# Two blocks of a feed-forward stage cut into slices of 4, 10, 12 and 6 steps, with accumulating stores, and a fixed order for the first attention block

## The chip, the cores and the metric

The kernel runs on one core of a Trainium2 chip. Its time is the device time of one execution in microseconds (us). Five engines run side by side, each with its own queue of instructions: TensorE (PE in the profile, PEld for its weight loads), VectorE (DVE), ScalarE (ACT), GpSimd (POOL) and SyncE (SP), which only issues DMA transfers here. DMA transfers are also issued from ACT's queue.

## The reference

A banded attention feeds a first feed-forward stage (FFN 1), and that a second one (FFN 2). What matters of it:

```python
# attention: 4 batches, 8 heads, 576 positions, 64 wide; 2304 tokens in all
scores = scale * q @ k.T; masked to a window of 32 (heads 0-3)
                          or to every 4th of 128 (heads 4-7)
attn = softmax(scores); x = attn @ v            # x: 2304 x 512
# FFN 1, d_ff 2048
h = x @ w_in
g = where(h > 0, h, exp(min(h, 0)) - 1)
x = g @ w_out
# FFN 2, d_ff 1536
out = ((x @ w_a) * (x @ w_b)) @ w_out2
```

All inputs arrive as float32.

## The kernel before

**Blocks and steps.** The tokens are cut into six blocks of 384 (`TB`). A block's x has four tiles, one for each pair of heads (p = 0 to 3, called head 0 to 3 from here on), and each is kept as a high and a low part. FFN 1 runs in steps (block t, slice f of 128 of the 2048 hidden columns), 16 slices for each block, 96 steps in all; the list `STEPS1` gives their order. A step s has an input pass `h1_mm` (12 matmuls of 128x384 into one of two `ps_h` banks, line 603; three for each tile of x, as high and low parts are combined), then `el` and `g` (ACT: relu and exp, lines 624 and 625; DVE: line 630; ACT and POOL split it into parts, lines 614 and 615), and two steps later its output pass `y1_mm` (12 matmuls into four `ps_y` banks, line 649). When the run of steps of one block ends, `y1_out` copies the four banks out.

**The order of the blocks.** The list runs block 0 through slices 0 to 6 (`SPLIT` = 7), block 1 through all 16, block 0 through slices 7 to 15, then blocks 2 to 5 whole. Block 0's first part is stored to a buffer `yp` in DRAM; `y_part_load` brings it back later, DVE adds it to the second part, and SP stores the sum. So block 1's steps 7 to 13 use slices whose weights are already in place.

**Weights.** A chunk of weights (1i f: the slice's input weights, 1o f: its output weights, 512 KB each) is loaded by `w_load` into one of four `wraw` buffers and converted: on ACT two passes (lines 273, 278), on DVE clamp, join and sign (lines 283, 288, 291), on ACT the high part (line 299), on DVE the low part (line 318). Chunks up to slice 7 (1i up to 9) are converted at a fixed place, two in each step, behind that step's g (`at_step(st, "C", w_convert, ...)`). The others are broken into single operations (`chunk_ops`); a planner (`tick`, two in a step) lets them out by a budget of each engine's time (`ROOM1` up to step `C0`, then `ROOM`), and after them the preparation of FFN 2's weights, which go back to DRAM.

**Attention of blocks 0 and 1.** For each head: `early_scores` (one mask matmul, line 407, and small matmuls, line 421), `early_exp` (kind "V": DVE takes the maximum and subtracts, ACT does one exponential; kind "A": DVE takes the maximum, ACT does six small exponentials with sums), `early_norm` (sum and reciprocal on DVE, the product on POOL, line 462), `early_transpose` (three transposes, line 470, and a copy on ACT, line 473) and `early_values` (small matmuls, line 488, into two `ps_a` banks of two; ACT takes the high part, line 503, DVE the low part, line 504). Block 0's four heads come before step 0 in a loop, shifted against each other. Block 1's heads are laid by the list `B1` into steps 0 to 6, those of block 2 by `B2` from step 18 on.

**What sets the order.** The engines' queues are in order; the order in them is chosen when the program is built, from the order in which the code is written and from when operands are expected. `tc.issue_after(x)` puts an instruction behind x on the same engine's queue, without a wait between engines. PE runs 11 matmuls on zeros ahead of the first scores (`warm`); `keep_warm` puts more of them around block 0's last two heads.

## Time and profile before

| | us |
|---|---|
| median of 3 runs | 906.41 (906.32 to 907.79) |
| the profiled execution | 904.56 |
| its span, first to last instruction | 902.5 |
| PE busy | 883.1 (98%) |
| DVE busy | 650.7 (72%) |
| ACT busy | 504.6 (56%) |
| POOL busy | 270.5 (30%) |

A row of the profile's timeline gives the start, the duration, the engine, the line of the kernel, the operation with the tiles that it writes and reads, the shapes, and the number of instructions; in brackets stands how long the engine sat idle ahead of it and what ended that. The duration of a row of matmuls counts the tail of the last one, so rows that follow each other overlap a little. PEclk is TensorE's granted clock as a share of 2.4 GHz.

### The profile page before, as it was taken

The numbers are of one execution on the slowest core, as the hardware profiler recorded it, in microseconds if no ns is written. First come the engines' busy times: TensorE is split into PE (matmuls) and PEld (weight loads), VectorE is DVE, ScalarE is ACT, GpSimd is POOL, SyncE is SP. The second block draws the span as 40 slices with busy tenths as digits, with TensorE's granted clock in tenths as the row PEclk, the third lists the DMA queues.
The fourth block names the chain that finished last, engine by engine and source line by source line (L and its number), as shares of the span: only waits on it lengthen the run. The fifth ranks groups of instructions, "written<-read, shape, count | busy, mean of one in ns | idle before, by whom it ended". The sixth has DMA issues, their size and how long they took to land.

```text
span 902.5 us, 17842 instructions
## 1 busy us (share of the span) xinstructions
PE 883.1 (98%) x6648; PEld 850.5 (94%) x6648; DVE 650.7 (72%) x1126; ACT 504.6 (56%) x1235; POOL 270.5 (30%) x252
## 2 busy tenths in 40 slices
PE   8989998999999999999999999999999999999998
PEld 5778998899999999999989999999999999999998
DVE  5899988777777776777865466689756689656666
ACT  5898787777677777676656342325342225343231
POOL 1132332333333333332222122222522222522233
PEclk8999999999999999999999999999999999999999
DMA  9575453748646655537996687766787754687722
GB/s 352 186 260 198 142 161 121 261 160 271 203 163 221 213 186 208 187 130 249 345 326 213 219 298 259 250 221 202 239 324 251 245 199 164 229 297 245 245 71 70
DMA packets 76245, 198.18 MB, mean 220 GB/s; under 512 B 8320, under 2 KB 22656, under 8 KB 76160
## 3 DMA queue, kind: packets, MB, share of 16 engines
q1 hardware_dynamic: 64064, 178.05, 58.3%
q10 hardware_dynamic: 12096, 19.01, 5.8%
q8 instruction: 52, 0.85, 0.4%
q14 instruction: 33, 0.27, 0.1%
HBM read 153.51 MB, written 43.52 MB: 218 GB/s over the span
## 4 chain that ended last, share of the span: by engine, by line
PE 81%; DVE 7%; ACT 2%; DMA 1%; issue 1%; ACTq 0%; SPq 0%; DVEq 0%
PE ps_h L1051 28%; PE ps_y L649 18%; PE ps_h L603 17%; PE ps_o L1380 14%; PE ps_v L586 1%; PE ps_s L550 1%; PE ps_t L570 1%; PE ps_o L1240 1%; DVE wt L288 1%; DVE wt L291 1%; DVE wraw L994 1%; DMA w<-w2Q__2948 1%; DMA w<-w2P_b 1%; ACT el L625 0%; DMA w2P_a<-wraw 0%
## 5 line engine op out<-in xcount | busy, mean ns | idle before, releaser
L1051 PE MATMUL ps_h<-y,w 128*128 128x384 f32 x1512 | 291.4, 336 | 0.0
L1051 PEld LDWEIGHTS ps_h<-y,w 128*128 128x128 f32 x1512 | 256.2, 188 | 2.1 <-DVE el L1106 0.6
L603 PE MATMUL ps_h<-x,w 128*128 128x384 f32 x1152 | 223.9, 340 | 4.1 <-DVE el L630 3.0
L649 PE MATMUL ps_y<-g,w 128*128 128x384 f32 x1152 | 223.0, 339 | 1.9 <-DVE w L318 0.8
L603 PEld LDWEIGHTS ps_h<-x,w 128*128 128x128 f32 x1152 | 198.7, 188 | 9.1 <-DVE el L630 4.2
L615 POOL TENSOR_TENSOR g<-el,g 128x384 fp32r<-128x384 f32 x96 | 116.5, 1214 | 298.4 <-ACT g L614 242.9
L649 PEld LDWEIGHTS ps_y<-g,w 128*128 128x128 f32 x1152 | 199.5, 188 | 5.9 <-DVE w L318 1.4
L1380 PE MATMUL ps_o<-w,g 128*128 128x256 f32 x1071 | 152.8, 281 | 1.3 <-DVE g L1168 1.3
L1380 PEld LDWEIGHTS ps_o<-w,g 128*128 128x128 f32 x1071 | 146.6, 188 | 2.0 <-DVE g L1168 1.8
L630 DVE SCALAR_TENSOR_TENSOR el<-el,ps_h 128x384 f32<-128x384 f32 x96 | 53.0, 552 | 80.1 <-ACT el L625 80.1
L624 ACT ACTIVATE el<-ps_h 128x384 f32<-128x384 f32 x96 | 46.7, 487 | 53.2 <-PE ps_h L603 49.5
L1093 POOL TENSOR_TENSOR g<-el,g 128x384 fp32r<-128x384 f32 x34 | 38.8, 1141 | 123.2 <-ACT g L1092 106.5
L1403 DVE TENSOR_TENSOR acc<-acc,ps_o 128x512 f32<-128x512 f32 (+1 forms) x77 | 49.6, 644 | 34.3 <-PE ps_o L1380 34.0
L288 DVE SCALAR_TENSOR_TENSOR wt<-wt,wraw 128x512 uint32<-128x512 uint32 x68 | 60.1, 889 | 3.3 <-ACT wraw L278 1.2
L291 DVE SCALAR_TENSOR_TENSOR wt<-wraw,wt 128x512 uint32<-128x512 uint32 x68 | 61.2, 905 | 0.9
L614 ACT ACTIVATE g<-el 128x384 fp32r<-128x384 f32 x96 | 49.6, 516 | 15.2 <-DVE el L630 15.2
L625 ACT ACTIVATE el<-el 128x384 f32<-128x384 f32 x96 | 50.2, 524 | 1.9
L278 ACT ACTIVATE wraw<-wraw 128x512 uint32<-128x512 uint32 x68 | 45.4, 669 | 6.7 <-issue 2.0
L273 ACT ACTIVATE wt<-wraw 128x512 f32<-128x512 f32 x68 | 44.8, 661 | 4.2 <-DMA wraw<-in_w1i 3.1
L1102 ACT COPY el<-ps_h 128x384 f32<-128x384 f32 x36 | 17.3, 479 | 53.3 <-PE ps_h L1051 51.0
L1141 DVE TENSOR_TENSOR u<-ps_h,u 128x384 f32<-128x384 f32 x36 | 20.0, 557 | 35.2 <-PE ps_h L1051 35.1
L1122 ACT COPY u<-ps_h 128x384 f32<-128x384 f32 x36 | 17.3, 480 | 47.2 <-PE ps_h L1051 47.2
(116 smaller groups left out, 1036.1 us busy)
## 6 DMA issues: line engine op xcount, KB each, us to landing
w<-w2P_o SPq DMA_DIRECT2D x52, 512.0 KB, 5.3
w<-w2P_a SPq DMA_DIRECT2D x48, 512.0 KB, 4.3
w<-w2P_b SPq DMA_DIRECT2D x48, 512.0 KB, 4.4
wraw<-in_w1i SPq DMA_DIRECT2D x16, 512.0 KB, 5.1
wraw<-in_w1o SPq DMA_DIRECT2D x16, 512.0 KB, 4.0
wraw<-in_w2a SPq DMA_DIRECT2D x12, 512.0 KB, 3.7
wraw<-in_w2b SPq DMA_DIRECT2D x12, 512.0 KB, 3.9
wraw<-in_w2o SPq DMA_DIRECT2D x12, 512.0 KB, 3.7
```

The costliest lines, as they stand in the source:

```text
L288: V.scalar_tensor_tensor(t, t, 3, L, op0=ALU.logical_shift_left, op1=ALU.bitwise_or)
L291: V.scalar_tensor_tensor(t, H, 0x80000000, t, op0=ALU.bitwise_and, op1=ALU.bitwise_or)
L603: T.matmul(ps[:, :TB], w[:, wi, kc * 128 : (kc + 1) * 128], xs[kc][:, xi, :], start=(n == 0), stop=(n == 3 * KC - 1),)
L614: A.activation(g[:, 0, :], gf, AF.Copy)
L615: G.tensor_tensor(g[:, 1, :], gf, f32(g[:, 0, :]), op=ALU.subtract)
L624: A.activation(e, ps[:, :TB], AF.Relu, scale=-1.0)
L625: last_e[0] = A.activation(e, e, AF.Exp, scale=-1.0)
L630: last_g[0] = V.scalar_tensor_tensor(e, e, -1.0, h_ps.pop(s)[:, :TB], op0=ALU.add, op1=ALU.max)
L649: T.matmul(y_ps[t][c][:, :TB], w[:, wi, c * 128 : (c + 1) * 128], g[:, gi, :], start=(first and n == 0), stop=(last and n == 2),)
L1051: last_mm[0] = T.matmul(ps[:, :TB], w[:, wi, kc * 128 : (kc + 1) * 128], y2[S, yop][kc][:, xi, :], start=(start and n == 0), stop=(n == 5) ...
L1380: T.matmul(ps[:, 256 * n : 256 * n + 256], g[name][:, gi, i * 128 : (i + 1) * 128], w[:, wi, h, :], start=((first or not held) and n == m ...
L1403: V.tensor_tensor(a, a, ps[:, :n], op=ADD)
```

## The change

The order of FFN 1's first two blocks becomes block 0 slices 0 to 3, block 1 slices 0 to 9, block 0 slices 4 to 15, block 1 slices 10 to 15. Chunks of slices 0 to 3 (1i up to 5) keep their fixed places, all others go to the planner, which starts at step 4. Block 1's attention is laid into steps 0 to 3 (`ATT1`: the step of scores, of transposes and of values for each head). In block 2, head 0 is turned at step 25 instead of 23 (`E2`).

`y1_out` treats all blocks alike: it copies the four banks to `el` buffers, two on ACT and two on DVE. The first part of a block is stored from SP and ACT as before; a second part is stored from POOL with an accumulating store onto the first part in DRAM. The buffers `yp`, `y_part_load` and the additions on DVE go.

Block 0's attention is written out in one order (`start_up`). `in_turn` puts what it calls behind the last instruction written so far on PE, ACT and DVE. In it the functions `early_exp`, `early_norm` and `w_convert` are cut into their parts (`top`: maximum, `less`: subtraction, `exp`; `total`: sum, `norm`: reciprocal and product) with the same operations. Head 3's product is on DVE instead of POOL, head 1's values go to `ps_y`, the low part of (1i, 0) comes behind head 3's product, and the load of (1i, 1) waits for a small memset that POOL does behind head 0's product. The keep-warm matmuls are 1, 7 and 3 wide ones at three places.

The core of the diff (left out: the cut of the three functions into parts, and the names of pools that follow from the new order):

```diff
-SPLIT = 7
-STEPS1 = [(0, f) for f in range(SPLIT)] + [(1, f) for f in range(NF1)]
-STEPS1 += [(0, f) for f in range(SPLIT, NF1)]
+FIRST_W = 7
+TURNS = (4, 10)
+STEPS1 = [(0, f) for f in range(TURNS[0])] + [(1, f) for f in range(TURNS[1])]
+STEPS1 += [(0, f) for f in range(TURNS[0], NF1)] + [(1, f) for f in range(TURNS[1], NF1)]
-KEEP_T, KEEP_V = 3, 1
+KEEP = (1, 7, 3)
...
-C1, C0, AHEAD, LAG_IN, LAG_OUT = SPLIT, NF1 + SPLIT, 56, 3, 2
+C1, C0, AHEAD, LAG_IN, LAG_OUT = TURNS[0], TURNS[0] + 18, 56, 3, 2
...
-CV1 = 4
-B1 = (-4, -2, 0, 2)
+WB_AT = 4
+ATT1 = [(0, 1, 1), (0, 1, 2), (0, 2, 2), (1, 2, 3)]
+E2 = (25, 26, 28, 30)
...
-    def w_load(key):
+    def w_load(key, behind=None):
         kind, f = key
         raw = pm.tile([128, 512, 2], U32, tag="wraw", name="wraw", bufs=NRAW)
+        if behind is not None:
+            with tc.issue_after(behind):
+                G.memset(raw[:, :1, 0], 0)
         SP.dma_start(
             out=raw.rearrange("p f h -> p (f h)"), in_=ins["w" + kind][f].bitcast(U32)
         )
...
-    def y1_out(t, whole):
+    def y1_out(t):
-            nm = f"y{t}_{i}" if whole else f"yp_{i}"
-            d = dr.tile([128, 2, TB], F32, tag=nm, name=nm)
-            add = t == 0 and whole
-            if add:
-                yp = y_part[i]
-                to = [yp[:, j, :] for j in range(2)]
-            else:
-                to = [pm.tile([128, TB], F32, tag="el", name="el", bufs=N_EL) for _ in range(2)]
-                stores += [(d[:, j, :], to[j], SP if j else A) for j in range(2)]
+            add = (t, i) in y_dr
+            if not add:
+                y_dr[t, i] = dr.tile([128, 2, TB], F32, tag=f"y{t}_{i}", name=f"y{t}_{i}")
+            d = y_dr[t, i]
+                to = pm.tile([128, TB], F32, tag="el", name="el", bufs=N_EL)
+                if j:
+                    V.tensor_copy(to, ps)
+                else:
+                    A.copy(to, ps)
-                    V.tensor_tensor(to[j], to[j], ps, op=ALU.add)
-                elif j:
-                    V.tensor_copy(to[j], ps)
+                    stores.append((G, d[:, j, :], to, {"accum_op": ALU.add}))
-                    A.copy(to[j], ps)
-            if add:
-                SP.dma_start(out=d, in_=yp)
-            y_dr[t if whole else "part", i] = d
-        for to, src, eng in stores:
-            eng.dma_start(out=to, in_=src)
+                    stores.append((SP if j else A, d[:, j, :], to, {}))
+        for eng, to, src, how in stores:
+            eng.dma_start(out=to, in_=src, **how)
-    def y_part_load():
-        for i in range(KC // 2):
-            yp = steady.tile([128, TB + LD], F32, "qk")[:, : 2 * TB]
-            yp = yp.rearrange("p (j n) -> p j n", j=2)
-            SP.dma_start(out=yp, in_=y_dr.pop(("part", i)))
-            y_part.append(yp)
...
+    PINNED = (mybir.EngineType.PE, mybir.EngineType.Activation, mybir.EngineType.DVE)
+    def in_turn(fn, *args):
+        with ExitStack() as stack:
+            for engine in PINNED:
+                traced = reversed(nc.cur_bb.bb.instructions)
+                last = next((i for i in traced if i.engine == engine), None)
+                if last is not None:
+                    stack.enter_context(tc.issue_after(last))
+            return fn(*args)
+    def keep_warm(n, to):
+        for _ in range(n):
+            T.matmul(to, zero[:, :128], zero, start=True, stop=True)
...
-    w_convert([("1i", 0)], "w", ON0)
+    *steps0, lower0 = w_convert_parts(("1i", 0), "w", ON0)
+    for step in steps0:
+        step()
...
-    for i in range(NP + 2):
-        if i < NP:
-            early_scores(0, i, ps_y, "y")
-            early_exp(0, i, EXP0[i])
-        if i == CV1:
-            w_convert([("1i", 1)], "w", ON1)
-        if i == NP - 1:
-            ps_k = ps_y.tile([128, 512], F32, tag="y", name="ps_k")
-        if 0 <= i - 1 < NP:
-            early_norm(0, i - 1)
-        if 0 <= i - 2 < NP:
-            p = i - 2
-            if i >= NP:
-                keep_warm(KEEP_T, True)
-            if i >= NP:
-                keep_warm(KEEP_V, False)
-            early_values(0, p)
+    def start_up():
+        top, less, exp, total, norm = ({} for _ in range(5))
+        def begin(p):
+            early_scores(0, p, ps_y, "y")
+            top[p], less[p], exp[p] = early_exp_parts(0, p, EXP0[p])
+            total[p], norm[p] = early_norm_parts(0, p)
+        def turn(p):
             early_transpose(0, p, A, ps_h, "h")
-            if i >= NP:
-                keep_warm(KEEP_V, False)
-            early_values(0, p)
+        def begin_values(p):
+            early_values(0, p, *((ps_y, "y") if p == 1 else ()))
+        ps_k = ps_a.tile([128, 512], F32, tag="a", name="ps_k")
+        in_turn(begin, 0)
+        in_turn(begin, 1)
+        for fn in (top[0], less[0], exp[0], top[1], less[1], exp[1]):
+            in_turn(fn)
+        in_turn(begin, 2)
+        for fn in (top[2], less[2], total[0], total[1]):
+            in_turn(fn)
+        in_turn(keep_warm, KEEP[0], ps_k)
+        in_turn(begin, 3)
+        in_turn(keep_warm, KEEP[1], ps_k)
+        in_turn(norm[0])
+        w_load(("1i", 1), behind=nc.cur_bb.bb.instructions[-1])
+        for fn in (top[3], exp[2], norm[1], less[3], total[2], exp[3], norm[2]):
+            in_turn(fn)
+        w_load(("1o", 0))
+        mask_load(2)
+        in_turn(turn, 0)
+        in_turn(keep_warm, KEEP[2], ps_k)
+        in_turn(turn, 1)
+        in_turn(total[3])
+        in_turn(norm[3], V)
+        in_turn(lower0)
+        in_turn(begin_values, 0)
+        in_turn(turn, 2)
+        in_turn(begin_values, 1)
+        in_turn(turn, 3)
+        high, low, clamp, *rest = w_convert_parts(("1i", 1), "w", ON1)
+        in_turn(high)
+        in_turn(begin_values, 2)
+        in_turn(low)
+        in_turn(clamp)
+        in_turn(begin_values, 3)
+        for fn in rest:
+            in_turn(fn)
+    start_up()
...
-        if f > SPLIT:
+        if f >= TURNS[0]:
...
-                end = b0 + 1 + int(b0 >= 0)
-                at_step(max(b0, 0), "A", early_scores, t, p)
-                at_step(max(b0, 0), "A", early_exp, t, p, EXP1[p])
-                at_step(max(b0, 0), "A", early_norm, t, p)
-                at_step(max(end + 1, 0), "B", early_transpose, t, p, A)
-                at_step(max(end + 2, 0), "B2", early_values, t, p)
+                at_step(b0, "A", early_scores, t, p)
+                at_step(b0, "A", early_exp, t, p, EXP1[p])
+                at_step(b0, "A", early_norm, t, p)
+                at_step(ATT1[p][1], "B", early_transpose, t, p, A)
+                at_step(ATT1[p][2], "B2", early_values, t, p)
-                end = b0 + 5 if t > EARLY else (23, 26, 28, 30)[p]
+                end = b0 + 5 if t > EARLY else E2[p]
...
-    at_step(NF1 + 13, "L2", held, y_part_load)
```

## Rows read from the trace of the kernel before

**Rows 1.** Busy time by stretch: us, PE, PEld, DVE, ACT, POOL, PEclk, DMA share, GB/s
```profile
24.50:57.70 33.20, 31.08 (x460) 25.65 (x453) 29.36 (x58) 28.20 (x78) 7.96 (x8) 1.00 0.64 216
...
85.35:143.28 57.93, 57.93 (x369) 57.09 (x369) 50.99 (x82) 46.19 (x107) 17.53 (x16) 1.00 0.45 143
143.28:180.00 36.72, 32.69 (x279) 29.69 (x278) 28.25 (x55) 27.05 (x84) 12.76 (x13) 1.00 0.61 209
```

**Rows 2.** Timeline of PE, 80 to 90 us
```profile
82.96 0.79 PE L649 MATMUL ps_y<-g,w 128*128 128x384 f32 x3 [0.45 <-DVE el L684]
83.59 1.92 PE L603 MATMUL ps_h<-x,w 128*128 128x384 f32 x10
...
89.51 2.24 PE L649 MATMUL ps_y<-g,w 128*128 128x384 f32 x12
```

**Rows 3.** Timeline of PE, the first 30 us
```profile
9.87 0.52 PE L421 MATMUL ps_s<-qk 64*32 64x64 f32 x18 [0.27 <-DMA qk<-in_qk_d]
12.33 0.55 PE L470 MATMUL ps_t<-ident,e 128*128 128x128 f32 x3 [1.94 <-POOL e L462]
...
18.05 1.46 PE L1437 MATMUL ps_k<-zero 128*128 128x512 bf16 x3
...
27.06 0.62 PE L603 MATMUL ps_h<-x,w 128*128 128x384 f32 x2
```

**Rows 4.** PE's groups by line, 24.5 to 85.35 us: count, busy us, mean ns, idle before
```profile
L603 PE MATMUL ps_h<-x,w 128*128 128x384 f32 x131 | 28.9, 351 | 1.1 <-ACT x L503 0.7 <-DVE x L504 0.4
L649 PE MATMUL ps_y<-g,w 128*128 128x384 f32 x97 | 21.2, 344 | 1.8 <-DVE w L318 0.8 <-ACT w L299 0.6 <-DVE el L684 0.4
L488 PE MATMUL ps_v<-pt,v 64*64 64x32 f32 x200 | 5.7, 221 | 0.0
```

**Rows 5.** Timeline of PE, 143 to 180 us
```profile
145.26 2.35 PE L603 MATMUL ps_h<-x,w 128*128 128x384 f32 x12 [1.17 <-DVE el L630]
...
151.66 1.29 PE L586 MATMUL ps_v<-pt,v 96*64 96x64 f32 x24 [1.55 <-ACT pt L573]
...
167.48 1.25 PE L550 MATMUL ps_s<-qk 64*64 64x128 f32 x24 [1.14 <-ACT pt L573]
```

**Rows 6.** DVE's groups by line, 24.5 to 85.35 us
```profile
L318 DVE TENSOR_TENSOR w<-wt,w 128x512 fp32r<-128x512 f32 x17 | 14.0, 835 | 0.6 <-ACT w L299 0.6
L288 DVE SCALAR_TENSOR_TENSOR wt<-wt,wraw 128x512 uint32<-128x512 uint32 x17 | 12.0, 732 | 0.4
L291 DVE SCALAR_TENSOR_TENSOR wt<-wraw,wt 128x512 uint32<-128x512 uint32 x16 | 12.0, 771 | 0.1
L283 DVE TENSOR_SCALAR wt<-wt 128x512 f32<-128x512 f32 x16 | 7.8, 511 | 0.5 <-ACT wt L273 0.5
...
L504 DVE TENSOR_TENSOR x<-ps_v,x 128x192 fp32r<-128x192 f32 x10 | 4.2, 443 | 1.6 <-ACT x L503 1.6
```

**Rows 7.** Busy time by stretch, as rows 1, in the start-up
```profile
10.00:12.00 2.00, 0.39 (x18) 0.22 (x14) 1.75 (x5) 1.97 (x13) 0.56 (x1) 1.00 1.06 411
...
14.00:16.00 2.00, 2.00 (x45) 1.69 (x42) 1.16 (x6) 0.77 (x3) 0.83 (x1) 0.50 1.05 409
...
20.00:22.00 2.00, 2.00 (x54) 1.48 (x54) 0.64 (x2) 0.61 (x2) 0.00 (x0) 0.82 1.02 399
```

**Rows 8.** Timeline of ACT, the first 30 us
```profile
12.91 0.48 ACT L473 COPY pt<-ps_t 128x384 f32<-128x384 f32 x1 [0.25 <-PE ps_t L470]
...
24.04 0.69 ACT L273 ACTIVATE wt<-wraw 128x512 f32<-128x512 f32 x1
...
25.17 0.88 ACT L503 ACTIVATE x<-ps_v 128x192 fp32r<-128x192 f32 x2
```

**Rows 9.** DMA issues up to 400 us: queue, count, KB each, median us to landing
```profile
wraw<-in_w1i SPq DMA_DIRECT2D x16, 512.0 KB, 5.1
...
y<-el ACTq DMA_DIRECT2D x6, 192.0 KB, 3.6
```

**Rows 10.** Timeline of DVE, 50 to 60 us
```profile
57.05 0.68 DVE L318 TENSOR_TENSOR w<-wt,w 128x512 fp32r<-128x512 f32 x1
```

More of the change, by code (lines that the diff above doesn't have):

```diff
@@ L429, in early_exp, with early_exp_parts @@
     def early_exp(t, p, by):
+        for part in early_exp_parts(t, p, by):
+            part()
+    def early_exp_parts(t, p, by):
         a = att[t, p]
@@ L447, in early_exp, with early_norm_parts, total, norm @@
                 )
[L448 to L451 removed]
+        return [top, less, exp]
     def early_norm(t, p):
+        for part in early_norm_parts(t, p):
+            part()
+    def early_norm_parts(t, p):
         a = att[t, p]
         e, (by, sm, rs) = a["e"], a["sums"]
[L456 to L462 removed]
+        def total():
+            if by == "A":
+                A.activation(rs, sm, AF.Copy, bias=1e-9)
+            else:
+                V.tensor_reduce(sm, e, axis=AX.X, op=ALU.add)
+                V.tensor_scalar(rs, sm, 1e-9, None, op0=ALU.add)
+        def norm(eng=G):
+            V.reciprocal(rs, rs)
+            eng.tensor_tensor(e, e, rs[:, :, None].to_broadcast([128, WN // 2, KN]), op=ALU.mult)
+        return [total, norm]
     def early_transpose(t, p, eng, pool=None, tag="a"):
@@ L475, in early_transpose, with early_values @@
             eng.tensor_copy(pt, ps)
-    def early_values(t, p):
+    def early_values(t, p, pool=None, tag="a"):
         a = att.pop((t, p))
         pt, v = a["pt"], a["v"]
-        ps = [ps_a.tile([128, 512], F32, tag="a", name="ps_v") for _ in range(2)]
+        ps = [(pool or ps_a).tile([128, 512], F32, tag=tag, name="ps_v") for _ in range(2)]
         ps = [x[:, : TB // 2].rearrange("p (s q) -> p s q", q=QN) for x in ps]
@@ L633, in h1_g, with pool_of @@
         split_g(s, e)
-    y_part = []
+    def pool_of(key):
+        return "w" if key[1] < FIRST_W + 2 * (key[0] == "1i") else "wb"
     def y1_parts(s):
@@ L1428, in banded_attention_two_ffn @@
     warm(WARM)
-    def keep_warm(n, wide):
-        traced = nc.cur_bb.bb.instructions
-        pe = next(i for i in reversed(traced) if i.engine == mybir.EngineType.PE)
-        with tc.issue_after(pe):
-            for _ in range(n):
-                if wide:
-                    T.matmul(ps_k, zero[:, :128], zero, start=True, stop=True)
-                    continue
-                for w in (256, 256, 192, 192):
-                    z = zero.bitcast(F32R)[:, :w]
-                    T.matmul(ps_k[:, :w], z[:, :128], z, start=True, stop=True)
+    PINNED = (mybir.EngineType.PE, mybir.EngineType.Activation, mybir.EngineType.DVE)
[10 more added lines that the diff above has]
+            T.matmul(to, zero[:, :128], zero, start=True, stop=True)
     first = steady.tile([128, 4], F32, "nm")
@@ L1491, in banded_attention_two_ffn @@
                 at_step(max(0, st - 1), "B" if f else "L", w_load, k)
-        at_step(st, "C", w_convert, ks, "w" if f < SPLIT else "wb", ON1)
+        at_step(st, "C", w_convert, ks, "w", ON1)
     def held(fn, *args):
@@ L1560, in w2_fetch_next @@
         for kind, f in freed(at):
-            n["w" if f < SPLIT + 2 * (kind == "i") else "wb"] += 1
+            n[pool_of(("1" + kind, f))] += 1
         for queue, src in ((fetch, free), (fetch_o, free_o)):
```

67 lines of the change are left out of this document (29 added, 38 removed).

## The prediction

> **What bounds the kernel now.** I read the table of stretches first. TensorE (PE) is the bound, but not everywhere. From 85.35 to 143.28 it is busy every microsecond [rows 1], and so it is behind 180 but for single waits; there a pass of 12 matmuls starts 2.08 us after the one ahead (89.51 and its neighbours, recorded as 2.24 with the tail of the last one) [rows 2], and nothing on another engine can shorten that. The change leaves the FFN matmuls alone, so it can only win back time that PE loses, and that sits in three places.
>
> (a) The start. The last two matmuls of step 0's pass run at 27.06 [rows 3] and end at 27.6.
> (b) 24.5 to 85.35. The lines view counts 131 + 97 FFN matmuls there [rows 4]: 228 x 2.08/12 = 39.5 us. Block 1's attention, with the rest of block 0's, takes PE about 9 us more (its values 5.7 us busy [rows 4], scores, masks and transposes 7.2, less the tails that each group's row counts in). 60.85 - 48.5 is 12 us lost. The stretch ends with step 10's pass, ten matmuls of it at 83.59 [rows 2].
> (c) 143.28 to 180. By the same count 30 of 36.7 us are work and some 6.5 are lost, 3.9 of them in three waits [rows 5].
>
> In (b) VectorE (DVE) sets the pace: 29.36 of the 33.2 us from 24.5 to 57.7 are busy [rows 1]. Converting one weight chunk costs it four instructions, 0.84 + 0.73 + 0.77 + 0.51 = 2.85 us [rows 6], a pair per step while steps 0 to 6 need new weights, 5.7 us beside a PE step of 4.16.
>
> **The start-up.** Before, three things stretch it. PE waits 1.94 us for POOL's product ahead of the first transposes at 12.33 [rows 3], busy for 0.39 us from 10 to 12 [rows 7]; after that the granted clock is 0.50, the 1.2 GHz level, from about 14 to some way past 20 [rows 7], so values and transposes run at half speed; and the keep-warm matmuls stand on the path itself, 3 wide ones from 18.05 ahead of head 2's values, with narrow ones behind them. Weight conversions of chunk 1i1 and 1o0 slip in between on ScalarE (ACT).
>
> After, PE, ACT and DVE follow one written order for this part. The first turn (transposes) still needs POOL's product, about 12.5, because the heads' loads and exponentials ahead of it are the same (head 3's q and k arrive at 9.87 [rows 3]). From the first copy at 12.9 ACT has in its order 4 copies of 0.48, 4 heads' high parts of 0.88 and 2 steps of 1i1's conversion of 0.69 [rows 8]: 1.9 + 3.5 + 1.4 = 6.8 us, to 19.7 without a gap. I add 1.6 us of gaps: head 3's values use the two ps_a banks that head 2's values hold until DVE has taken its low part. Head 3's high part is then done at 21.3, its low part (0.44 a half [rows 6]) at 21.7, and step 0's pass at 22.2 instead of 27.6: **-5.4**. Bounds: -7 with no gap; -2.5 if the clock falls again as it did, since the four heads' values and transposes then take twice their 1.2 us, most of it inside the chain.
> The 11 new keep-warm matmuls stand ahead of the second turn, where PE has nothing else; three of the kind take 1.46 us at half clock [rows 3], so 11 take some 2.7 at full clock, and they fill the hole of 1.94. That is why I take the clock as held. The Trainium skill, "TensorE: Matmul & The Clock Gate", "Part 1: The HAM clock gate", says that an idle stretch halves the clock and dense activity gives it back; the fall behind that hole agrees. By that rule the term stays at -5.4.
> Head 3's normalisation goes from POOL to DVE and (1i,0)'s low part moves behind it: both stand beside ACT's chain of 6.8 us, the longer one, so they are hidden; without that cover, +0.55 each. The load of 1i1 now waits for a small POOL memset behind the first product, and every later load waits behind it in SP's queue. The first 4 MB (heads and values) are on their way by then and get the DMA engines alone; 1i1 lands some 5 us after its issue [rows 9], near 17, ahead of its conversion. Cost 0; if 1o0 and block 1's heads come late, up to +2.
>
> **Steps 0 to 10.** Before, block 1 (x1) is due at step 7, after 14 converted chunks; now at step 4, after 8, but with the same attention of block 1 ahead of it. I size it by a stretch that did nearly the same: from 24.5 to 57.7 DVE finished 9 chunks (the last, 1i5, at 57.05 [rows 10]), 5 steps' g, all scores of block 1 and 6 of the low halves. After, from 21.7 until x1 is there it has some 8.5 chunks, 4 steps' g, the same scores and 8 low halves: equal within a microsecond, 33 us. So x1 is there at 54.7, and step 4's pass ends at 55.2. From there no new chunk is due for four steps, and the planner's chunks come one pair a step (3.7 us of DVE's 4.16 with g), as they do without loss in 85 to 143 [rows 1]. Left until step 10's pass has ended are 6 input passes and 5.5 to 6 output passes of 2.08: 24 us, 79 to 80. Before it ends at 85.35, so the two parts together give **-5.5**; the shape of the slices alone gives about nothing here, because DVE's work per PE step ahead of x1 becomes larger (attention over 4 steps, not 7), while the steps behind it become free. Bounds: -9 if DVE's idle time of 3.8 us in that stretch goes; +1 if its instructions are as slow beside POOL as the longest ones of the trace.
>
> **The later turns.** There are four block turns instead of three, each with a wait like the 0.45 us at 82.96 [rows 2]: **+0.5**. Block 1's last slices (10 to 15) and their conversions now end near step 23 instead of 21, due 25 to 27 instead of 22 to 24; head 0 of block 2 is turned two steps later. Loss (c) hangs on ACT and DVE queues that are full of conversions, softmax and g at once, and that remains. I take **-1**, between -5 (the three waits gone and what they cost around them) and +3 (another half of today's loss, as chunks overlap more of block 2's softmax).
> The accumulating stores: 8 of 192 KB on POOL, in place of 2 loads and 2 stores on SP and four DVE additions (two of each four become ACT copies). No row shows an accumulating store or any store from POOL. Between "as today's" (3.6 us to landing [rows 9]) and one at a time at twice that, I take the first: the five el buffers hold four stores, the next user of a held one comes three passes, 6.2 us, after the last matmul, and PE itself stops only when both ps_h banks wait, 4.2 us later. So **0**, with up to +16 below.
>
> **Sum.** -5.5 + 0.5 - 1 = -6.0 on the profiled execution's 904.56 us (span 902.5): 898.6. The median of the runs shown is 906.41, 1.85 above that execution; so 900.5.
>
> **Rivals.**
> 1. The start-up's clock falls all the same. PE's work from 7 to 14 is small matmuls on a part of the array, as before. Then -2.5 instead of -5.4: 903.5. For it: the clock fell then. Against it: the hole is filled.
> 2. The stalls of (c) go too, and DVE is better packed: -9 and -4, 893. For it: ps_t and ps_v waits on ACT's copies make up 2.7 of its 3.9 us [rows 5], and head 0's turn, one of them, moves. Against it: planner and softmax keep DVE and ACT as full.
> 3. Slower: the accumulating stores hold the el buffers. Place: the turns at steps 27 and 33. Landing one after the other at 2 x 3.65 us, the fourth buffer is free after 29 us, where the steps want it at 6.2 + 3 x 4.16 = 18.7, with 4.2 more of slack: some 6 to 8 us a turn, 12 to 16 in both, 906 to 917 with the rest of the sum. It decides from 3 us a turn on, that is when a turn's last store lands more than 26 us behind its matmul. The Trainium skill, "SBUF — State Buffer", "SBUF: two separate sides", has a rule for this: GpSimd writes the descriptors of its own DMAs, and VectorE instructions in a two-port mode lock it out meanwhile. No row here shows it; by it the stores come late in just those steps where DVE is full, on the side of this rival. Against it: DVE is busy for only 28.25 of the 36.72 us from 143 to 180 [rows 1].
> 4. x1 is late, one long PE wait at step 4: no gain if x1 comes at 61 instead of 54.7, 906.4. For it: all DVE work of steps 0 to 3 is queued ahead, in program order.
>
> **How the numbers follow.** Forecast (897 to 903.5) 0.47; rival 1 0.13; rival 2 0.14; rival 4 0.12; rival 3 or another loss 0.14. A difference under 0.2% (1.8 us) can't be told from none. Faster takes the forecast, rival 2 and most of rival 1: 0.72. Same, 904.6 to 908.2, is mostly rival 4: 0.13. Slower 0.15. The range 893 to 909 leaves out the end of rival 2 and most of rival 3.
>
> **What would show it.** Right: granted clock 1.00 from 12 to 22; step 0's pass ends at 21 to 23.5; x1's last low part near 55; step 10's pass ends at 78 to 82; no PE wait of over a microsecond behind the turns at steps 27 and 33; the stores from POOL land within 6 us. Wrong: clock 0.50 in the start-up (rival 1), PE waits for el buffers or ACT's el instructions near 170 or 195 (rival 3), a wait for x1 beyond 60 (rival 4).

## The result, and the profile after

The changed kernel takes 917.36 us (median of 4 runs, 916.28 to 920.27) against 906.37 for the kernel before on the same chip; the ratio is 1.0145 with a 95% interval of 1.0121 to 1.0169. The medians differ by 11 us; by the ratio, which all runs below are judged by, the change makes the kernel 13 us slower, where 6 us faster was forecast. The profiled execution took 916.28 us (span 914.5).

Where the time goes is best read step by step. The table gives the start of DVE's `el` instruction of each step of FFN 1 (line 630 before, 661 after; one instruction per step) as the difference from the kernel before; the first column is that kernel's own time. Positive is late. The slices of a step differ between the two, but the number of passes done is the same. The other columns are experiments that are told below.

```
step  before | after  e2_room e17_room_w2 e16_before_w2 | e8_fixed2 e15_..shift | e12_..less e14_..shift e13_before_shift
   0    29.1 |  -0.7    +1.4      +0.5        +4.5      |   +0.1       +1.2     |   +1.7       +0.7        +1.5
   4    56.6 |  +5.5    +7.6      +6.0        +4.5      |   +5.6       +5.5     |   +1.7       +0.8        +1.4
  10    88.2 |  -5.2    -0.2      -1.8        +3.3      |   -2.3       -2.4     |   +0.7       +0.3        +1.0
  16   114.2 |  +0.3    +2.9      +1.5        +3.4      |   -1.4       -1.7     |   -1.3       -1.7        +0.9
  22   144.7 |  +0.9    +2.6      -1.2        +2.4      |   -3.6       -3.9     |   -4.6       -5.1        +0.5
  28   174.3 |  +4.7    +2.5      -1.9        -0.4      |   -3.3       -2.2     |   -3.5       -3.9        +5.2
  36   214.6 |  +6.3    +3.8      +0.2        -1.4      |   +3.1       -1.7     |   -1.7       -3.6        +4.2
  64   350.2 |  +6.4    +3.9      +0.8        -1.0      |  +13.5       -0.8     |   +8.5       -2.7       +14.8
  80   428.4 |  +6.0    +5.1      -0.1        -2.1      |  +16.2       -0.3     |  +11.2       -2.7       +16.9
  95   492.0 |  +9.7    +3.3      +4.3        +1.6      |  +19.3       +0.4     |  +12.2       -0.8       +19.7
```

The changed kernel is 5.2 us ahead at step 10, as wanted, and then loses 5.5 by step 16, 6.0 more by step 36 and 3.7 between steps 80 and 95; FFN 2 adds some 2. Two cautions. DVE's `el` can lie off PE's passes: step 10's pass ends 3.6 us earlier than before, its `el` comes 5.2 earlier. And a column is a single execution: at step 0 the eight kernels with the old start-up lie between 0.0 and +4.5, the twelve with the new one between -1.0 and +1.4.

**The start-up** (PE of the changed kernel; answers to [rows 3]; the last row is a DMA queue from 17 to 18 us, with packets, MB and share):

```profile
17.11 0.55 PE L519 MATMUL ps_v<-pt,v 64*64 64x32 f32 x22
19.60 0.59 PE L519 MATMUL ps_v<-pt,v 64*64 64x32 f32 x26 [1.95 <-issue]
...
22.98 1.97 PE L634 MATMUL ps_h<-x,w 128*128 128x384 f32 x5
24.75 0.54 PE L415 MATMUL ps_s<-m,m 128*128 128x384 bf16 x1
24.84 0.89 PE L634 MATMUL ps_h<-x,w 128*128 128x384 f32 x2
...
q8 instruction: 1, 0.02, 5.8%
```

PE stops for 1.95 us in the middle of head 2's values, with no wait that the profile shows ("issue"). As the stop begins, the DMA queue that the profile names "instruction" moves one packet of 16 KB; PE goes on 1.5 us after it has landed. Step 0's pass ends at 25.7, against 27.6 before; its `el` starts only 0.7 us earlier.

**Stretches** (columns as in [rows 1]), the changed kernel and then the kernel before:

```profile
12.00:20.00 8.00, 5.82 (x163) 4.18 (x161) 5.46 (x16) 4.02 (x10) 2.48 (x4) 1.00 0.87 300
...
22.00:24.00 2.00, 2.00 (x38) 1.94 (x34) 1.64 (x4) 1.72 (x5) 0.00 (x0) 0.50 1.04 414
...
60.00:67.00 7.00, 7.00 (x42) 7.00 (x41) 2.49 (x5) 5.50 (x13) 1.98 (x2) 1.00 0.34 122
90.00:120.00 30.00, 27.36 (x158) 24.85 (x160) 26.54 (x42) 22.66 (x44) 7.37 (x6) 1.00 0.58 177
140.00:180.00 40.00, 34.28 (x257) 31.26 (x256) 29.19 (x55) 27.77 (x84) 14.26 (x14) 0.96 0.36 102
...
162.00:164.00 2.00, 2.00 (x9) 1.99 (x8) 1.40 (x3) 1.64 (x8) 0.00 (x0) 0.50 0.63 194
...
496.80:500.40 3.60, 3.59 (x13) 3.59 (x14) 0.55 (x1) 1.95 (x4) 1.75 (x2) 0.58 0.21 57
```

```profile
60.00:67.00 7.00, 5.51 (x36) 4.73 (x37) 7.00 (x14) 6.39 (x14) 2.15 (x1) 1.00 0.69 239
90.00:120.00 30.00, 30.00 (x190) 29.63 (x189) 26.21 (x39) 23.93 (x47) 8.49 (x7) 1.00 0.47 145
140.00:180.00 40.00, 35.97 (x298) 32.92 (x297) 31.53 (x61) 30.19 (x95) 14.03 (x14) 1.00 0.58 198
```

From 60 to 67 DVE is busy for 2.49 of 7 us, where it had been full: block 1's x is there (its last low part, below), and no chunk is let out yet. From 90 to 120 PE, which had never stopped there, is busy for 27.36 of 30.

```profile
59.49 0.50 DVE L535 TENSOR_TENSOR x<-ps_v,x 128x192 fp32r<-128x192 f32 x1
```

The timeline of PE in the changed kernel says for what it waits (answers to [rows 2] and [rows 5]; L304 and L945 are the high and the low part of a chunk of the planner):

```profile
57.87 0.44 PE L634 MATMUL ps_h<-x,w 128*128 128x384 f32 x1 [2.02 <-ACT x L534]
...
79.66 2.24 PE L634 MATMUL ps_h<-x,w 128*128 128x384 f32 x12
...
92.80 3.12 PE L634 MATMUL ps_h<-x,w 128*128 128x384 f32 x14 [0.49 <-ACT w L304]
96.56 1.68 PE L682 MATMUL ps_y<-g,w 128*128 128x384 f32 x8 [0.64 <-ACT w L304]
...
105.49 0.97 PE L682 MATMUL ps_y<-g,w 128*128 128x384 f32 x4 [0.84 <-DVE w L945]
111.06 0.96 PE L682 MATMUL ps_y<-g,w 128*128 128x384 f32 x4 [0.35 <-DVE w L945]
...
146.17 2.35 PE L634 MATMUL ps_h<-x,w 128*128 128x384 f32 x12 [1.54 <-DVE el L661]
...
160.58 0.87 PE L581 MATMUL ps_s<-qk 64*64 64x128 f32 x12 [3.15 <-ACT pt L604]
...
162.20 3.41 PE L634 MATMUL ps_h<-x,w 128*128 128x384 f32 x10
```

The four waits for weights add up to 2.3 us; the 5.7 us by which PE's busy time from 140 to 180 falls short of 40 (4.0 before) include 3.15 for one copy on ACT. That wait costs twice: from 162 to 164 the granted clock is 0.50, the lower of its two levels, where it was 1.00 before, and ten matmuls take 3.41 us where twelve take 2.24 at 79.66. The last chunk of FFN 1 is finished late, beside block 2's softmax (DVE, changed kernel; before, its row starts at 139.55):

```profile
156.34 0.68 DVE L945 TENSOR_TENSOR w<-wt,w 128x512 fp32r<-128x512 f32 x1
```

**The end of FFN 1.** ACT, and behind it PE, changed kernel; then ACT and PE of the kernel before:

```profile
491.13 0.48 ACT L655 ACTIVATE el<-ps_h 128x384 f32<-128x384 f32 x1
495.04 0.65 ACT L283 ACTIVATE wraw<-wraw 128x512 uint32<-128x512 uint32 x1 [3.43 <-DMA wraw<-in_w2o]
495.60 0.51 ACT L656 ACTIVATE el<-el 128x384 f32<-128x384 f32 x1
```

```profile
496.81 3.73 PE L634 MATMUL ps_h<-x,w 128*128 128x384 f32 x12 [3.54 <-DVE el L661]
...
502.50 1.23 PE L1065 MATMUL ps_h<-y,w 128*128 128x384 f32 x6
```

```profile
478.42 0.67 ACT L278 ACTIVATE wraw<-wraw 128x512 uint32<-128x512 uint32 x1
...
492.46 1.23 PE L1051 MATMUL ps_h<-y,w 128*128 128x384 f32 x6
```

The preparation of FFN 2's weights comes behind the last chunk of FFN 1. SP's first store of it is issued at 176.63, in step 27, instead of 151.59, in step 23, and the last second pass of a conversion runs on ACT at 495.04 instead of 478.42, among the last steps of FFN 1. There it stands ahead of `el` in ACT's queue (L656 behind L283) and waits 3.43 us for its load; PE waits as long, and its next pass, at a granted clock of 0.58, takes 3.73 us instead of 2.24.

Between step 10's pass (3.6 us ahead) and its first matmul of FFN 2 (502.50 against 492.46, 10.0 behind) PE loses 13.6 us. Its stops from 85 to 180 (8.2 us against 3.9 before), the two slow stretches (some 1.5 each) and the 3.54 at the end make up 10.8 of them.

**The accumulating stores** (DMA issues of the first 400 us, columns as in [rows 9], and POOL's timeline):

```profile
y<-el ACTq DMA_DIRECT2D x8, 192.0 KB, 3.5
y<-el SPq DMA_DIRECT2D x8, 192.0 KB, 3.8
y<-el POOLq DMA_DIRECT2D x8, 192.0 KB, 5.7
```

```profile
174.87 2.80 POOL L719 DMA_DIRECT2D y<-el  x3
180.55 0.88 POOL L719 DMA_DIRECT2D y<-el  x1 [2.88 <-DVE wt L296]
```

```profile
211.03 0.49 ACT L655 ACTIVATE el<-ps_h 128x384 f32<-128x384 f32 x1 [3.02 <-POOL g L646]
```

At the second of these turns ACT's `el` waits 3.02 us for a `g` that POOL makes between its stores (last row); PE does not stop there.

### The profile page after: what moved, and what is told of

Same layout as the page of the kernel before. It is cut to its first block, busy times and chain, and to the rows that moved or that the text cites. A ratio compares the mean times of both kernels' runs of the same rounds, so it can differ in the third digit from the quotient of the medians.

```text
span 914.5 us, 17854 instructions
## 1 busy us (share of the span) xinstructions
PE 885.1 (97%) x6643; PEld 851.8 (93%) x6645; DVE 647.8 (71%) x1127; ACT 507.6 (56%) x1239; POOL 275.9 (30%) x260
## 4 chain that ended last, share of the span: by engine, by line
PE 74%; DVE 11%; DMA 7%; ACT 5%; issue 2%; POOL 0%; SPq 0%; ACTq 0%; DVEq 0%; POOLq 0%
PE ps_h L1065 27%; PE ps_h L634 15%; PE ps_y L682 14%; PE ps_o L1394 13%; DVE wt L293 2%; DVE wt L296 2%; PE ps_v L617 1%; DMA wraw<-in_w1o 1%; DMA wraw<-in_w2o 1%; DVE wt L288 1%; ACT el L656 1%; PE ps_t L601 1%; PE ps_o L1254 1%; PE ps_s L581 1%; DVE el L661 1%
## 5 line engine op out<-in xcount | busy, mean ns | idle before, releaser
L634 PE MATMUL ps_h<-x,w 128*128 128x384 f32 x1152 | 228.0, 344 | 9.5 <-DVE el L661 5.8
L634 PEld LDWEIGHTS ps_h<-x,w 128*128 128x128 f32 x1152 | 202.6, 191 | 14.3 <-DVE el L661 6.8
L296 DVE SCALAR_TENSOR_TENSOR wt<-wraw,wt 128x512 uint32<-128x512 uint32 x68 | 63.6, 938 | 0.8
L645 ACT ACTIVATE g<-el 128x384 fp32r<-128x384 f32 x96 | 49.6, 516 | 9.2 <-DVE el L661 8.9
L283 ACT ACTIVATE wraw<-wraw 128x512 uint32<-128x512 uint32 x68 | 45.1, 669 | 14.9 <-DMA wraw<-in_w2o 6.1
L656 ACT ACTIVATE el<-el 128x384 f32<-128x384 f32 x96 | 50.3, 525 | 3.2 <-issue 1.1
L278 ACT ACTIVATE wt<-wraw 128x512 f32<-128x512 f32 x68 | 44.7, 660 | 10.8 <-DMA wraw<-in_w1i 3.6
L1116 ACT COPY el<-ps_h 128x384 f32<-128x384 f32 x36 | 17.3, 480 | 50.6 <-PE ps_h L1065 50.6
L1106 ACT ACTIVATE g<-el 128x384 fp32r<-128x384 f32 x36 | 18.9, 524 | 44.2 <-DVE el L1124 37.4
```

What stands on the lines that cost most here:

```text
L296: V.scalar_tensor_tensor(t, H, 0x80000000, t, op0=ALU.bitwise_and, op1=ALU.bitwise_or)
L634: T.matmul(ps[:, :TB], w[:, wi, kc * 128 : (kc + 1) * 128], xs[kc][:, xi, :], start=(n == 0), stop=(n == 3 * KC - 1),)
L645: A.activation(g[:, 0, :], gf, AF.Copy)
L656: last_e[0] = A.activation(e, e, AF.Exp, scale=-1.0)
```

## The experiments

Each ran beside the kernel before, on the same chip as the others of its group (medians of before 903.9 to 905.1). The theories are named by letters in the expectations. A: the planner's list lets chunks of a later need ahead of those that are due. B: the accumulating stores. C: the planner's pace, its budget, is too low. D: the stretch without chunks from step 4 to 8. E, formed later: where FFN 2's weight preparation lies.

### Which part of the change

**e4_plain**: the second parts are stored plainly to a buffer that nothing reads, so the two parts are not added.

```diff
+            if add:
+                d = dr.tile([128, 2, TB], F32, tag=f"z{t}_{i}", name=f"z{t}_{i}")
...
-                    stores.append((G, d[:, j, :], to, {"accum_op": ALU.add}))
+                    stores.append((SP if j else A, d[:, j, :], to, {}))
```

> The changed kernel with the eight accumulating stores replaced by plain stores from SP and ACT into buffers that nobody reads (so the two parts of blocks 0 and 1 are not added). Theory B (accumulating stores hold the el buffers or POOL): the loss goes with them, 906 to 911. Theories A and C (the conversions): 916 to 918, since PE showed no wait of over a microsecond behind the steps with these stores, and they landed 5.7 us after their issue.

918.11 us, ratio 1.0143 (1.0109 to 1.0177), the change's own. The accumulating stores cost nothing in all; B falls.

**e5_old_slices**: the new start-up and stores with the old slices and places.

```diff
-TURNS = (4, 10)
+TURNS = (7, 16)
...
-C1, C0, AHEAD, LAG_IN, LAG_OUT = TURNS[0], TURNS[0] + 18, 56, 3, 2
+C1, C0, AHEAD, LAG_IN, LAG_OUT = TURNS[0], TURNS[0] + 16, 56, 3, 2
...
-ATT1 = [(0, 1, 1), (0, 1, 2), (0, 2, 2), (1, 2, 3)]
+ATT1 = [(0, 0, 0), (0, 0, 1), (0, 3, 4), (2, 5, 6)]
...
-E2 = (25, 26, 28, 30)
+E2 = (23, 26, 28, 30)
...
```

> The new start-up alone: slices in the old order (7, 16, 9), block 1's attention, the planner's start and its budget, and block 2's head 0 as before; the fixed order of the first block's attention stays, and block 0's second part still goes by accumulating stores. Theories A and C (the new slices cost the time): the start-up's gain of about 2 us is left, 903 to 906. Theory B: the four accumulating stores that are left cost about half of the loss, 909 to 912. If the start-up itself is what costs: 912 to 917.

905.45 us, ratio 1.0009 (0.9990 to 1.0029). The start-up brings nothing that can be measured. PE stops at the same instruction, and the clock falls behind it:

```profile
17.23 0.54 PE L519 MATMUL ps_v<-pt,v 64*64 64x32 f32 x22
20.01 0.59 PE L519 MATMUL ps_v<-pt,v 64*64 64x32 f32 x26 [2.23 <-issue]
```

The stop does not belong to the new start-up. All twelve kernels with it have the stop, 1.95 to 2.53 us long, behind the 346th to 348th matmul that the profile records; of the eight with the old one four have it at the same count, 2.64 to 2.83 us long, one has 0.73 us there, and in three, the kernel before among them, PE reaches that matmul only at 20.88 or later. In all twenty a 16 KB packet of the "instruction" queue lands 1.2 us or more before the next matmul starts. So a faster start-up runs into this point; no run moves it, so the cause is not shown. The stop in e12_before_less, which has the old start-up:

```profile
21.98 0.54 PE L488 MATMUL ps_v<-pt,v 64*64 64x32 f32 x19 [2.64 <-issue]
```

**e6_old_start**: the new slices with the old loop for block 0's attention.

```diff
-    start_up()
+    for i in range(NP + 2):
+        if i < NP:
+            early_scores(0, i, ps_y, "y")
...
```

> The new slices alone: the old loop over the first block's attention with its keep-warm matmuls, everything else as in the changed kernel. Theories A and C: the start-up's gain is lost, 918 to 921. If the fixed order of the start-up costs time further on (SP's loads waiting behind the memset): 910 to 915.

919.42 us, ratio 1.0162 (1.0131 to 1.0192). The loss belongs to the slices.

### Order and pace of the chunks

**e1_due** sorts the planner's chunks by the step that needs them.

```diff
...
-            for k in ks[::-1]:
-                chunk_ops(k)
+            late += ks[::-1]
...
+    for k in sorted(late, key=due):
+        chunk_ops(k)
```

> The changed kernel, with the planner's weight chunks listed by the step at which they are due, so that 1o8 and 1o9 (due at steps 14 and 15) come ahead of 1i10 and 1i11 (due at 20 and 21). Theory A (the planner's order starves PE): the waits of PE for converted weights between 90 and 112 us go, 3.5 to 4.5 us, and the time falls to 911 to 914; the losses from 140 to 170 and near 495 stay, since the number of chunks and their pace are the same. Theory B (the accumulating stores cost the time): nothing changes, 917. Theory C (the pace of conversions, not their order, is short): the waits stay or move by a step, 916 to 918.

913.0 us, ratio 1.0097 (1.0060 to 1.0134): some 4 of the 13 us come back. It was 3.9 us ahead of the kernel before at step 24 and lost 9.5 by step 36.

**e2_room** raises the planner's budget, nothing else; **e3_due_room** does both.

```diff
-ROOM1 = {"V": 1.6, "A": 1.3, "G": 0.9}
+ROOM1 = {"V": 2.1, "A": 1.7, "G": 0.9}
```

> The changed kernel with a larger budget for the planner up to step 22 (2.1 us of DVE and 1.7 of ACT a tick instead of 1.6 and 1.3), the order of chunks as it is. By the written order the last first-stage chunk is then done at step 22 instead of 25, and the second stage's weights begin at step 22 instead of 27. Theory C (the pace is short: the chunks and everything behind them come late): the waits at 90 to 112 shrink to under 2 us, the wait of 3.5 us near 496 goes, 907 to 911. Theory A (only the order of the chunks): 915 to 918. If DVE and ACT have no room for more, g comes late everywhere: 918 to 925.

906.1 us, ratio 1.0016 (0.9997 to 1.0035): 11 us come back. The last chunk of FFN 1 starts its last operation at 141.98, behind `el` of step 21, instead of 156.34, behind that of step 24.

> Both: chunks by the step at which they are due, and the larger budget. Theories A and C add up: no wait of PE for weights behind 70 us, 905 to 909. If the loss between 140 and 170 (block 2's softmax beside conversions) is a matter of its own: 909 to 912.

906.78 us, ratio 1.0025 (1.0003 to 1.0047): with the pace right, the order adds nothing. C explains more than A. The program shows the shortage too: where a chunk is due and not let out, `need` runs the planner on beyond its two ticks a step. That happens four times in the changed kernel, for 1o 7, 8 and 9 at steps 13 to 15, once in e1_due, and not in e2_room or e3_due_room.

**e8_fixed2** converts slices 4 and 5 at fixed places, chunks by due step, planner from step 5; **e9_fixed2_room** is that with the larger budget.

```diff
-C1, C0, AHEAD, LAG_IN, LAG_OUT = TURNS[0], TURNS[0] + 18, 56, 3, 2
+C1, C0, AHEAD, LAG_IN, LAG_OUT = 5, TURNS[0] + 18, 56, 3, 2
...
-        if f >= TURNS[0]:
+        if f >= TURNS[0] + 2:
...
```

> Chunks by due step, and two more slices (4 and 5) converted at fixed places in steps 4 and 5, with the planner starting at step 5 instead of 4, its budget as in the changed kernel. In the changed kernel DVE stands idle for some 5 us between 59 and 67, because the planner's first chunks have to be loaded and let out first. Theory D (that start-up gap of the planner is the lost time): DVE's idle time there goes, the waits at 90 to 112 go, and all that follows comes two steps earlier, 906 to 910. Theories A and C without D: as with the order alone, 912 to 914.

> Chunks by due step, slices 4 and 5 at fixed places, and the larger budget: the last first-stage chunk at step 20, the second stage's weights from step 20 on, earlier than in the kernel before (22 and 23). If lateness of conversions is the whole loss: 899 to 905, at or below the kernel before. If block 2's attention beside the turns at steps 20 and 26 costs by itself: 906 to 911.

923.79 (ratio 1.0221, 1.0186 to 1.0255) and 931.75 us (1.0307, 1.0266 to 1.0348). Both lie above every range that was set; as a cure, D falls. But the table shows e8 3.6 us ahead at step 22; its 23 us are lost behind that, up to step 95, and PE's timeline shows no wait for a weight of FFN 1 there. So pace was not all.

**Budget as a dose.** e10_before_room and e12_before_less are the kernel before with 2.1 / 1.7 and 1.4 / 1.14, e11_mid and e13_more the changed one with 1.85 / 1.5 and 2.6 / 2.1.

> The kernel before, with the planner's larger budget alone (2.1 / 1.7 instead of 1.6 / 1.3). Theory C (the budget matters only where the written order lets a chunk come after its step needs it): before's 14 planned chunks already came in time, so 903 to 907. Rival (the larger budget is a gain by itself, worth the 11 us that it gave in the changed kernel): 893 to 897.

> The kernel before, with a smaller budget (1.4 / 1.14): its last planned chunk is written at step 24 instead of 22, as the change did to it with the old budget (25). Theory C: the same kind of loss without any of the change's slices, PE waits for the planner's weights at 100 to 150 us, 909 to 914. Rival (the loss needs the slices themselves): 904 to 907.

> The changed kernel with a budget half way (1.85 / 1.5); last chunk at step 23, between the change's 25 and 22 of the larger one. Theory C with a loss that grows with the lateness: 910 to 913. Rival (a single wait somewhere that either happens or doesn't): near 906 or near 917.

> The changed kernel with a still larger budget (2.6 / 2.1); last chunk at step 19. Theory C: nothing is late any more at 2.1 but single waits at 101 to 115 us, 2.5 us in all, so 903 to 906. Rival (with more operations let out at once they stand ahead of g, softmax and copies on DVE and ACT): 908 to 915.

Measured: 907.22 (ratio 1.0025), 919.14 (1.0152), 915.37 (1.0114), 916.16 (1.0124). The larger budget is no gain by itself. The changed kernel gives 917.4, 915.4, 906.1 and 916.2 for budgets 1.6, 1.85, 2.1 and 2.6: no smooth dose. With 2.6 no weight is late, and PE waits for POOL's `g` three times between 90 and 130, for 5.1 us in all:

```profile
93.44 2.20 PE L682 MATMUL ps_y<-g,w 128*128 128x384 f32 x11 [2.59 <-POOL g L646]
```

And e12 is slower, as C said, but 5 us beyond C's range and for another reason: it was 4.6 us ahead at step 22 and lost 12.8 between steps 40 and 80.

### The place of FFN 2's weight preparation

It repeats every eight ticks (four steps), and so does the attention of blocks 3 to 5 (four steps a head). e12 and e8 lose in that stretch with the first chunk of a pair loaded ahead of `g` of steps 44, 48, ...; before, it is loaded behind `g` of 45, 49, .... Three runs move these loads alone, by holding them:

```diff
...
+                return not FROM <= now[0] < LATE or now[0] % 8 == (PHASE + 4 * (f % 2)) % 8
...
-            a = Op("D", 0, load, takes="wraw")
+            a = Op("D", 0, load, takes="wraw", gate=gate if key[0][0] == "2" else None)
```

> The kernel before, every chunk of FFN 1 as it was; only the loads of FFN 2's weights are held until another place of the planner's cycle of eight ticks (four steps): the first chunk of a pair at the tick ahead of g of steps 44, 48, ... instead of the one behind g of 45, 49, ..., as in the run with the smaller budget. Theory E (where that cycle stands against the attention's cycle of four steps sets whether ACT reaches a conversion before its load has landed): 10 to 14 us lost in steps 40 to 80, 914 to 920. Rival (late chunks of FFN 1 are what costs): 904 to 908.

924.53 us, ratio 1.0218 (1.0181 to 1.0255).

> The kernel before with the smaller budget (919.1), and the loads of FFN 2's weights held until the place in the cycle that they have in the kernel before (behind g of steps 45, 49, ...). Theory E: the 12 us of steps 40 to 80 come back, 905 to 910 with the end of that preparation two steps later. Rival (late chunks): 917 to 921, nothing changes.

904.2 us, ratio 1.0004 (0.9982 to 1.0026).

> The changed kernel with slices 4 and 5 at fixed places and the chunks by due step (923.8), which was 5.6 us ahead of the kernel before at step 26, and the loads of FFN 2's weights held until the place in the cycle that they have in the kernel before. Theory E: the 13 us of steps 40 to 80 come back, 908 to 913. Rival (this order of FFN 1's chunks is what costs): 921 to 926.

906.2 us, ratio 1.0018 (1.0001 to 1.0035). Three times the place alone moved the time by 15 to 20 us, in both directions and with either set of slices. Stretch 260 to 470 (columns as in [rows 1]) before, then in e13_before_shift, then in e14_less_shift:

```profile
260.00:470.00 210.00, 208.16 (x1503) 200.72 (x1503) 153.95 (x266) 147.93 (x375) 63.90 (x59) 1.00 0.66 224
```

```profile
260.00:470.00 210.00, 199.14 (x1435) 189.06 (x1435) 146.01 (x258) 142.41 (x375) 65.03 (x57) 1.00 0.59 199
```

```profile
260.00:470.00 210.00, 207.78 (x1500) 200.09 (x1499) 154.97 (x267) 147.31 (x372) 62.58 (x58) 1.00 0.65 223
```

How it costs, on ACT and then PE of e13_before_shift (L274 and L279 are the first two passes of a conversion, L389 the softmax, L574 the copy of the transposes):

```profile
315.72 0.66 ACT L274 ACTIVATE wt<-wraw 128x512 f32<-128x512 f32 x1 [1.85 <-DMA w2P_b<-wt]
...
322.65 0.68 ACT L279 ACTIVATE wraw<-wraw 128x512 uint32<-128x512 uint32 x1 [1.17 <-DMA wraw<-in_w2a]
...
324.35 0.66 ACT L274 ACTIVATE wt<-wraw 128x512 f32<-128x512 f32 x1 [0.92 <-DMA w2Q__3797<-wt]
324.91 0.39 ACT L389 ACTIVATE e<-e,nm 128x128 f32<-128x128 f32 x1
...
330.20 0.46 ACT L574 COPY pt<-ps_t 128x384 f32<-128x384 f32 x1
```

```profile
330.72 0.91 PE L587 MATMUL ps_v<-pt,v 128*64 128x64 f32 x22 [1.94 <-ACT pt L574]
```

ACT's queue reaches a conversion before its load, or the store that frees its buffer, is through; softmax and copy stand behind it, and PE behind the copy. In all, ACT waits for DMAs for 31 us between 180 and 500 in this run, 1.9 us before, 5.2 in e14_less_shift, and 17.3 in the changed kernel. The sum is a sign and not a price: e17_room_w2 has 19.6 and loses 6.6 in all.

The twenty kernels together say more of the place than the cycle of four steps. In the order in which the programs are written, fourteen let these loads out behind a step's `g`; from step 40 to 80 they lose between -0.9 and +1.4 us. Six let them out ahead of `g`: four of these ahead of even steps (e12, e8, e9 and e13_before_shift), and they lose 10 to 14 us; e13_more and e1_due, ahead of odd steps, lose 0.4 and 2.0. Only the three runs above move the place alone, so this pattern is read from the runs and not tested.

**e16_before_w2** holds these loads in the old kernel until the tick numbers that they have in the changed kernel, counted from step 0; **e17_room_w2** does so in e2_room.

```diff
+            if now[0] < self.first:
+                return False
...
-            a = Op("D", 0, load, takes="wraw")
+            a = Op("D", 0, load, takes="wraw", first=W2_AT.get(key, 0))
```

> The kernel before with its own slices, start-up and FFN 1 chunks; only each load of FFN 2's weights is held until the step at which the changed kernel issues it (first one at step 22 as there, the later ones 3 to 7 steps later than before). Theory E, for the change itself (what costs behind step 22 is where this preparation lies): 4 to 5 us lost in steps 22 to 40 and 4 to 6 from step 80 on, 912 to 916. Rival (the slices and the late chunks cost by themselves): 904 to 907.

904.4 us, ratio 0.9991 (0.9970 to 1.0012): in the old kernel the later preparation costs nothing in all.

> The changed kernel with the larger budget (906.1), its FFN 1 chunks as early as there, and each load of FFN 2's weights held until the tick that it has in the changed kernel itself (6 to 16 ticks later). Theory E: most of the gain of the larger budget goes again, 913 to 917. Rival (the larger budget helps because FFN 1's chunks come earlier): 905 to 908.

909.78 us, ratio 1.0073 (1.0047 to 1.0100), between the two expectations. Neither run has the place that it was meant to have. The changed kernel's four extra ticks put its tick numbers two steps ahead of its steps, so the held loads come later than there: the fifth load of `in_w2a` is issued in step 41 before, in step 45 in the changed kernel, and in step 47 in both runs.

By the ratios, each against the kernel before of its own runs, the changed kernel loses 13.1 us, e17_room_w2 6.6 and e2_room 1.4, each known to some 2 us. The last two differ by the preparation alone, but by one that lies two steps later than the changed kernel's, so the loss can't be divided by them. The table tells where each part falls. From step 10 to 36 the changed kernel loses 11.5 us, e17_room_w2, with its preparation later still, 2.0, and e2_room 4.0: a late preparation does not cost here, so this part belongs to the pace of FFN 1's chunks. Between steps 80 and 95 the three kernels with the late preparation lose alike, 3.7 (changed), 4.4 (e17) and 3.7 (e16), where e2_room gains 1.8. e16_before_w2 loses nothing in all, as it is 2.1 us ahead at step 80.

**e18_less_late3** is e14_less_shift with the last lag shortened.

```diff
-LATE, LAG_LATE = 2 * (NF1 * (NB - 1) - C1), 7
+LATE, LAG_LATE = 2 * (NF1 * (NB - 1) - C1), 3
```

> The kernel before with the smaller budget and the preparation moved back to its old place (904.2, 5 us ahead at step 22 and 2.7 ahead through steps 40 to 80), with the lag of its last loads at 3 ticks instead of 7, so that it ends one step earlier. If the 2 us that were lost behind step 80 come from that end: 902 to 903.5. Else 904 to 906.

905.87 us, ratio 1.0005 (0.9985 to 1.0024): no gain. No version beat the kernel before.

## Why the prediction was wrong

**The start-up, -5.4 forecast, -1.9 measured.** The turns and ACT's copies came some 0.6 us later than said (first turn at 13.04), and the granted clock held at 1.00 from 12 to 20. Then came a stop that no step of mine had, 1.95 us inside head 2's values, and the clock fell all the same: 0.50 from 22 to 24. That is rival 1's fall behind another hole. Its price, -2.5, was about right. As the old start-up varies by more than this gain (0.0 to +4.5 at step 0), e5_old_slices shows nothing of it. The rule of the Trainium skill ("TensorE: Matmul & The Clock Gate", "Part 1: The HAM clock gate") held: the fall follows the idle stretch, as it does behind the waits of 3.15 and 3.54 us at 160.58 and 496.81.

**Until x1 is there, 33 us forecast.** From head 3's low part at 24.4 to x1's last one at 60.0 it took 35.6, so x1 came 5.3 us later than forecast. Step 10's pass, forecast to end at 79 to 80, ends at 81.7, against 85.35 before: 3.6 of 5.5 us.

**The step that failed** is "the planner's chunks come one pair a step ..., as they do without loss in 85 to 143", and with it the term of the later turns, -1 (bounds -5 to +3), which measured about +14: on PE from 3.6 us ahead at step 10 to 10.0 behind where FFN 2 begins. The step contradicts its own price: a pair at 2.85 us a chunk is 5.7 us of DVE, more than the 4.16 of a step, and its 3.7 are about one chunk with `g`. The rows that it leans on show that pace: from 85.35 to 143.28, 14 steps of 4.16, the kernel before finishes 14 chunks, one a step. Two things were overlooked, and both could be worked out from the code and the rows. First, the budget of 1.6 us a tick, 3.2 a step, lets out 1.14 chunks a step at 4 DVE operations that the planner counts at 0.7 each, not two. Before, 18 of 32 chunks had fixed places and 14 came from the planner; now it is 10 and 22. With a pace set by the budget, the lead at step 10 was a loan: by then 13 chunks stood in DVE's order, before 18, and DVE had been left idle from 60 to 67. e2_room, which changes the budget alone, brings 11 us back. Second, what follows the chunks in the planner, FFN 2's weights, moves with them. I had named the end of FFN 1's chunks ("near step 23 instead of 21") but priced nothing behind it. The wait of 3.43 us at 495.04 shows where a part of it falls; how the 13 us divide between the two is not isolated by any run. Nor did the prediction price what a long wait does to the clock, some 1.5 us each time.

**The accumulating stores, 0 forecast.** Right. Each takes POOL 0.9 us or more to issue and 5.7 us to land, within the 6 that I had set, and replacing them changes nothing; rival 3 is refuted, though its range (906 to 917) came close to the result. The Trainium skill's rule ("SBUF — State Buffer", "SBUF: two separate sides") says that VectorE can hold up such stores; here they are slower by 1.9 to 2.2 us than the plain ones, for a reason that no run isolates, and PE does not wait for them. (In e17_room_w2 one `el` on ACT waits 2.23 us for a buffer that such a store holds, at 209.59, which is that rival's mechanism.)

**Rival 4**, a late x1, came in part: x1's last low part lay at 60.0, near its 61. But PE's one long wait, 2.02 us, ended at 57.87, and step 10's pass still came 3.6 us early, so its price, no gain, did not follow.

**Open.** What makes a load ahead of an even step's `g` dear is not isolated; e11_mid, which looks like e12 and e8 in the cycle, is no exception, as its one extra tick puts its loads behind `g` of step 43 and not ahead of that of 44. Not settled either are the division of the loss between pace and preparation, 2.8 of PE's 13.6 us, what stops PE at 17.66, and why the largest budget (e13_more) loses most of its time behind step 28.

## What to carry to other kernels

When work is moved from fixed places to a planner with a budget, divide the budget by the cost of a piece and compare the pace with the need, and ask what comes behind it in the planner; a lead gained by not doing work yet is no gain. Where two periodic streams share in-order queues, their phase alone can be worth 2%: before a change is judged by its time, move the phase alone in the old kernel, as a control. A right sign is not a confirmed cause: the run with the smaller budget was slower, as expected, but in a stretch and by a mechanism that the expectation had not named. And a run that holds work until a counter of the program should be read in the trace first: ticks were not steps here, and two controls stood two steps off.

## What the runs showed of the hardware

- In 16 of 20 profiles PE stopped for 1.95 to 2.83 us behind its 346th to 348th recorded matmul, with no semaphore shown and the DMA engines full (share 0.94 to 1.03 from 17.6 to 19.6 us in the changed kernel, e2_room and e5_old_slices), and went on 1.2 to 1.6 us after a 16 KB packet of the "instruction" queue had landed.
- Each of three stops of PE in the changed kernel (1.95, 3.15 and 3.54 us) was followed by a granted clock of 0.50, where it had been 1.00; ten matmuls at 162.20 took 3.41 us.
- A store of 192 KB from POOL with accumulation landed in 5.7 us (median of 8), plain ones from ACT and SP in 3.5 and 3.8. Its issue took POOL 0.88 us or more.
- One instruction of ACT that waits for a load holds everything behind it: 3.43 us on ACT became 3.54 us on PE at 496.81.
